# Attention loop in which projections and output products run as pairs in halves of the array's rows

## The chip, the cores and the metric

The kernel runs on one core of a Trainium2 chip. The metric is the device time of one execution in microseconds (us), the median of several runs. A profile of one execution stands beside the times. Its engines are PE (TensorE, matrix products; PEld is its loading of stationary operands), DVE (VectorE), ACT (ScalarE), POOL (GpSimd) and SP (SyncE, which issues most of the DMAs).

## The reference

Four layers, A, B, A, B, act on x (2048 rows of 512), each after a layer norm and with the input added. Layer A is linear attention over learned features. Layer B, which the change touches, cuts the rows into four segments of 512 and attends within each segment, with a memory of the segments before:

```python
for s in range(N):                                   # N = 4 segments, H = 32 heads of 16
    qs, ks, vs = q[:, :, s], k[:, :, s], v[:, :, s]
    logits = einsum("bhqd,bhkd->bhqk", qs, ks) * scale + mask
    a_dot = einsum("bhqk,bhkd->bhqd", softmax(logits), vs)
    pq = phi(qs)                                     # phi(t) = t + 1 if t > 0, else exp(t)
    a_mem = einsum("bhld,bhde->bhle", pq, M) / (einsum("bhld,bhd->bhl", pq, z)[..., None] + 1e-6)
    outs.append(g * a_mem + (1 - g) * a_dot)         # g = sigmoid(beta), one for each head
    pk = phi(ks)
    M = M + einsum("bhld,bhle->bhde", pk, vs)
    z = z + einsum("bhld->bhd", pk)
return concat(outs) @ wo
```

q, k, v are the normed x times wq, wk, wv (512 by 512).

## The kernel before

All products of 512 by 512 weights are split into a high and a low part of each operand, so that each of the four chunks `kc` of the contraction takes three products of 128 rows, 128 columns and 512 moving columns (`mm3`, 12 products a job). A quarter of a job is one `kc`, three products.

Layer B is a loop of steps (`LayerB.steps`). There are 32 values of m a layer, eight for each segment: m picks one of four chunks c of 128 channels (eight heads) and one of two halves of it. Each m takes R = 5 steps, so step k belongs to m = k // 5. A step issues, in this order on each engine:

- `attend(m)`: scores of some blocks into the tile `lg` (two PSUM banks), as pairs of products of 64 rows (`tile_position` 0 and 64) that write different banks; ACT's exponential into a tile of tag `P4` (shown as P); POOL's mask of the diagonal;
- `maxima`, for a later m: pairs of products of 63 rows into `mx` and `my` (a bank each), from which DVE takes row maxima (`mxs`);
- in one step of some m, `read`: the memory's part for a chunk, into `pv` and a bank of tag `g`, which ACT copies to `old` and `upper` (shown as ot and mmq);
- functions put off from the steps before (`later`, `late`), and between them, in steps 0 and 2 of each m, `weighted`: the value sums of the m before, in strips of 32 columns of the array into `pv`, from step 2 on copied by ACT to U; and `update`, the memory's sums of four token blocks, a bank of tag `g`, which DVE adds to the memory. In step 2 the put-off lists come in the other order;
- what the table names for this step.

The tables FIRST (segment 0), GAPS (segments 1 and 2), LAST and FINAL (segment 3 of the first and second layer B) are an order written by hand. An entry `2.3 k3/2~` means: in step 3 of the segment's third m, two quarters of the k projection of chunk 3; a plus sign means the next segment's; `~` puts what DVE does at the job's end off to the next step's list `late`. `q`, `k` are projections, `v` value products, `out` the former segment's output products (four token blocks), `max` turns the maxima and stores them into Q (tile mt), `t` turns features of k to token order, `m` updates the memory, `a` reads it, `x` asks for the rows to which an output is added, `n` and `ln` advance a layer norm (`ln` are its transposes), `w` and `load` bring data, `p`, `pre`, `pt`, `fin` and a bare `v` belong to the end of the layer and to the layer after.

A projection's end (`proj`) is ACT's copy of the high part, DVE's subtraction for the low part, and for the feature map two ACT functions, an exponential and a Relu (`first`, `second`), one or two steps later. A value job ends with an ACT copy, an output with DVE's addition. All of these read the job's bank of tag `g`. There are G = 3 banks of that tag; `lg` has two, `mx`, `my` and `pv` one each, eight in all. Jobs, transposes and the update take a bank of `g` in program order.

`queue_w` loads the next weights of a projection, 512 KB, when one is done; two such tiles (`w4`) are held. `stack(m)` copies projected q and k by six DMAs to the tiles of the scores, in step 0 of the m three before. `Ordered` and `held` keep the order of the program on each engine.

Of the kernel before, what the change touches and what calls it, by code (L numbers as in the profile page):

```python
# [7 lines left out]
F32 = mybir.dt.float32  # L8
# [8 lines left out]
H = 32  # L17
DH = 16
P = 128
# [58 lines left out]


FIRST = """  # L80
0.1 max k2/2 | 0.2 v3/2 | 0.3 k2/2~ | 0.4 v3/2
1.0 m0 | 1.1 max q3/2 | 1.3 q3/2~ | 1.4 t1 k3/1
2.1 max k3/3 | 2.2 m1 w | 2.3 ln~ | 2.4 ln~ ln~
3.1 ln~ max | 3.3 q0+/2 | 3.4 t2 q0+/2~ w
4.0 w | 4.1 max k0+/2 load | 4.2 m2 | 4.3 k0+/1 | 4.4 k0+/1
5.0 n | 5.1 max v0+/4 | 5.2 w | 5.3 q1+/2 n | 5.4 t3 q1+/2~
6.1 max v1+/4 | 6.2 m3 n | 6.3 k1+/2 | 6.4 a0+ k1+/2
7.0 n | 7.1 max q2+/4~ | 7.2 n | 7.3 v2+/2 n | 7.4 t0+ v2+/2
# [12 lines left out]
LAST = """  # L101
0.1 max k2/3~ | 0.2 n | 0.3 k2/1~ v3/2 n | 0.4 a1 v3/2 n
1.0 n | 1.1 max q3/3 n | 1.2 n | 1.3 q3/1~ k3/2 n | 1.4 k3/2~ n
2.1 max out/1 | 2.3 out/2 | 2.4 a2 x0 pre
3.1 max ln~ ln~ | 3.3 pre out/1 ln~ out/1 x1 | 3.4 out/1 ln~
4.1 max out/2~ v/2 | 4.3 pre out/3 x2 | 4.4 a3 out/1~ v/2 x3
5.1 max out/3 | 5.2 out/1 v/1 | 5.3 fin v/1 | 5.4 v/2 pre
6.1 max v/2 | 6.3 fin v/2 | 6.4 v/2
7.1 pt p/3 v/2 | 7.2 v/2 | 7.3 fin v/2 p/3 | 7.4 p/3
"""  # L110
FINAL = """
0.1 max k2/4~ | 0.3 v3/3 | 0.4 a1 v3/1~
1.1 max q3/2 | 1.3 q3/2~ | 1.4 k3/1
2.1 max k3/2 | 2.3 k3/1 out/1 pre | 2.4 a2 out/2 x0
3.0 x1 | 3.1 max | 3.3 pre out/2 | 3.4 out/2
4.1 max out/1~ | 4.3 pre out/2 x2 | 4.4 a3 out/2
5.1 x3 out/2 max | 5.3 fin out/2 | 5.4 pre
6.1 max | 6.3 fin
7.1 pt p/2 | 7.3 p/4 fin | 7.4 p/3
"""  # L120
BEFORE = {-25: "q0 load", -23: "v0", -21: "k0", -18: "n", -17: "v1 n", -16: "n", -15: "n n", -14: "q1 n", -13: "n", -12: "k1 n n", -10: "v2 n", -4: "max q2~", -1: "t0"}


@with_exitstack
def interleave_kernel(ctx, tc, x_in, a_wqkv, a_wphi, a_wo, b_wq, b_wk, b_wv, b_wo, b_beta,
# [15 lines left out]
    def nm(s):  # L141
        uid[0] += 1
        return f"{s}_{uid[0]}"
# [4 lines left out]
    def PS(tag, bufs, shape=(P, 512)):  # L148
        return ps.tile(list(shape), F32, tag=tag, bufs=bufs, name=nm(tag))
# [14 lines left out]
    def behind(i, j):  # L164

        tc.add_manual_dep(i.ins, j.ins.name,
                          mybir.DependencyInfo(mybir.DependencyClass.NoSync, mybir.DependencyReason.DATA),
                          reason="keeps order")

    class Ordered:  # L170

# [36 lines left out]
    def dma(out, in_):  # L208
        return sync.dma_start(out=out.bitcast(F32), in_=in_.bitcast(F32))
# [15 lines left out]
    gated = cp.tile([P, NC, 4], F32, name="gated")  # L225
    ones = cp.tile([32, P], F32, name="ones")
    stats = cp.tile([P, NT, 4], F32, name="stats")
    junk = cp.tile([P, 2, 384], mybir.dt.uint8, name="junk")

    def constants():  # L230
# [776 lines left out]
    class LayerB:  # L1007
# [21 lines left out]

        def values(self, s):  # L1030

            self.vv[s] = []
            yield from v_tile(self.hT[s], self.wv, self.vv[s], ("g", G), (0, 3, 1, 2), True)

        def queue_w(self):

            if self.wnext:
                m, c = self.wnext.pop(0)
                w = wp.tile([P, 2, NC, P], F32R, tag="w4", bufs=2, name=nm("wqk"))
                dma(w, wqk[m][:, c])  # L1040
                self.w4.append(w)

        def proj(self, s, c, m):

            d, hT, w = self.st.setdefault((s, c), {}), self.hT[s], self.w4.pop(0)
            pp = PS("g", G)
            yield from mm3(pp, lambda a, kc: w[:, a, kc, :], lambda b, kc: hT[b][:, kc, :])
            self.queue_w()
# [15 lines left out]
            yield  # L1064

        def at(self, k, f, *a):

# [351 lines left out]

        def out(self, s):  # L1420
            for t in range(4):
                po = PS("g", G)
                yield from self.product(po, s, t, range(NC))

                def end(po=po, t=t):
                    x = self.xq.pop(0)
                    dve.tensor_tensor(out=x, in0=po, in1=x, op=ADD)
                    sync.dma_start(out=self.xdst[4 * s + t], in_=x)
                wait(end)
                yield  # L1430

        def early(self):

# [18 lines left out]
                yield  # L1452

        def opening(self):
            self.w4 = []
            self.wo = []
            self.wnext = [(m, c) for _ in range(NSEG) for c in range(NC) for m in range(2)]
            for _ in range(2):
                self.queue_w()
                yield  # L1460
            self.wv = []
            yield from bring(self.wv, "bwv")
            self.norm0 = self.norm(0)
            next(self.norm0)
            fills = self.start()
            for n in (0, 0, 1, 0, 1, 0, 1, 1, 1, 1, 0, 1, 1, 1, 1, 1, 1, 1, 1):
                yield
                next(self.norm0 if n else fills, None)

        def steps(self, side, after, table_end):  # L1470
# [8 lines left out]
            outs, proj, part = {}, {}, {}  # L1479
            early = self.early()  # L1480

            def do(what, s, k):
                put_off[0] = self.late if what[-1] == "~" else None
# [8 lines left out]
                elif op == "fin":  # L1492
                    if k >= FINAT:
                        self.finish((k - FINAT) // R)
                elif op in ("q", "k", "v", "out", "p"):
                    if op == "p":
                        g = early
                    elif op == "out":
                        if s == 0:
                            return  # L1500
                        g = outs.setdefault(s, self.out(s - 1))
                    elif op == "v":
                        g = after if i is None else val[s]
                    else:
                        g = proj.setdefault((s, i, op), self.proj(s, i, "qk".index(op)))
# [161 lines left out]
```

## Time and profile before

| | us |
|---|---|
| median of 3 runs (1403.53 to 1404.76) | 1403.86 |
| span of the profiled execution | 1401.3 |
| PE busy | 1369.1 |
| DVE busy | 963.9 |
| ACT busy | 810.9 |
| POOL busy | 734.1 |
| first layer B, first to last score product | 292.4 to 713.9 |
| second layer B, first to last score product | 979.0 to 1385.6 |

Matrix products are pipelined and their ends are modelled, so that a busy PE isn't one at its peak: what a product costs is read from one start to the next. The granted clock of TensorE was 1.00 throughout. In the profile's rows, a group stands as output<-inputs by the program's names, with rows by columns of the array and shape, the number of instructions, their busy time, the mean of one, and the idle time of the engine before them with what ended it.

### The profile page before, as it was taken

How to read it: one execution, taken by the hardware profiler on the slowest of the kernel's cores; microseconds unless marked ns; L12 is line 12 of the kernel's file. 1: busy time of each engine (PE TensorE's matmuls, PEld its weight loads, DVE VectorE, ACT ScalarE, POOL GpSimd, SP SyncE). 2: the span in 40 equal slices, each digit the busy share in tenths (PEclk: the TensorE clock that was granted, in tenths of full speed). 3: DMA queues.
4: the chain of work that ended last, by engine and by line, in shares of the span. 5: the costliest groups of instructions: out<-in, count | busy, mean ns of one | idle time of the engine just before them, and what ended most of it. 6: DMA issues, size and time to landing. Idle time of an engine off the chain costs nothing.

```text
span 1401.3 us, 33234 instructions
## 1 busy us (share of the span) xinstructions
PE 1369.1 (98%) x12070; PEld 943.2 (67%) x12070; DVE 963.9 (69%) x3030; ACT 810.9 (58%) x1244; POOL 734.1 (52%) x1073
## 2 busy tenths in 40 slices
PE   9999999999999999999999999999999999999998
PEld 7787778766666666655568887886655666666554
DVE  5766888677667657667647768958776666666674
ACT  5555445447686677566544434553566866765654
POOL 1677755324656656554534346642356565754643
PEclk9999999999999999999999999999999999999999
DMA  5369285645756656567631104855465566565552
GB/s 199 118 216 330 99 280 175 187 122 162 201 131 190 169 137 183 158 171 196 197 134 39 62 31 125 275 162 155 137 172 171 148 178 180 143 172 142 155 158 69
DMA packets 135730, 225.27 MB, mean 161 GB/s; under 512 B 21328, under 2 KB 39888, under 8 KB 135568
## 3 DMA queue, kind: packets, MB, share of 16 engines
q1 hardware_dynamic: 134464, 222.91, 54.2%
q8 instruction: 97, 1.59, 0.5%
q14 instruction: 65, 0.53, 0.1%
q10 hardware_dynamic: 1104, 0.24, 0.1%
HBM read 116.39 MB, written 43.25 MB: 114 GB/s over the span
## 4 chain that ended last, share of the span: by engine, by line
PE 78%; DVE 8%; ACT 5%; POOL 4%; issue 2%; DMA 2%; SPq 0%; DVEq 0%; ACTq 0%; POOLq 0%
PE g L202 47%; PE pv L202 9%; PE lg L202 9%; PE mx L202 4%; PE g L206 3%; PE my L202 3%; ACT P L180 2%; PE lg L206 1%; POOL P L180 1%; POOL tb L180 1%; DVE es L180 1%; POOL tmp L180 1%; DVE junk L180 1%; DVE my L180 1%; DVE mx L180 1%
## 5 line engine op out<-in xcount | busy, mean ns | idle before, releaser
L180 ACT ACTIVATE P<-lg 128x1024 f32<-128x1024 f32 x316 | 324.5, 1027 | 167.5 <-PE lg L202 159.6
L180 POOL TENSOR_SCALAR_AFFINE_SELECT P<-P 128x256 f32<-128x256 f32 (+1 forms) x448 | 190.3, 439 | 388.9 <-ACT P L180 388.1
L180 DVE CUSTOM_DVE_ANT_0 junk<-mx,mask 128x128 uint8<-128x128 f32 (+2 forms) x384 | 146.6, 420 | 101.8 <-PE my L202 72.7
L202 PE MATMUL g<-hh,wqk 128*128 128x512 f32 x512 | 186.3, 411 | 0.7 <-ACT mt L180 0.7
L202 PE MATMUL lg<-e,e 64*128 64x512 f32 (+1 forms) x1010 | 166.0, 386 | 6.4 <-ACT P L180 6.0
L180 DVE CUSTOM_DVE_ANT_0 mx<-mx,mask 128x512 f32<-128x512 f32 x128 | 89.2, 697 | 120.1 <-PE my L202 95.4
L202 PE MATMUL g<-w,oh 128*128 128x512 f32 x508 | 169.2, 414 | 0.5 <-ACT hh L180 0.4
L202 PE MATMUL pv<-P,v 128*32 128x512 f32 (+3 forms) x2048 | 165.5, 439 | 0.6 <-ACT ot L180 0.5
L202 PE MATMUL my<-e,e 63*128 63x256 f32 (+3 forms) x519 | 147.2, 343 | 4.2 <-DVE mxs L180 3.0
L202 PEld LDWEIGHTS lg<-e,e 64*128 64x128 f32 x1010 | 79.9, 184 | 102.9 <-issue 44.9
L202 PE MATMUL mx<-e,e 63*128 63x256 f32 (+3 forms) x519 | 145.9, 334 | 1.9 <-DVE mxs L180 1.6
L180 DVE CUSTOM_DVE_ANT_0 junk<-my,mask 128x128 uint8<-128x128 f32 (+2 forms) x384 | 146.8, 420 | 0.0
L202 PE MATMUL g<-w,hh 128*128 128x512 f32 x448 | 143.9, 402 | 0.3 <-ACT hh L180 0.3
L202 PEld LDWEIGHTS pv<-P,v 128*32 128x32 f32 x2048 | 53.5, 109 | 102.9 <-issue 95.3
L202 PEld LDWEIGHTS g<-hh,wqk 128*128 128x128 f32 x512 | 96.2, 188 | 33.7 <-issue 13.4
L202 PEld LDWEIGHTS g<-w,oh 128*128 128x128 f32 x508 | 87.6, 189 | 30.8 <-issue 13.4
L202 PE MATMUL g<-w,ol 128*128 128x512 f32 x254 | 100.8, 397 | 2.3 <-DVE ol L180 2.2
L180 DVE DVE_READ_ACCUMULATOR2_ANT mxs<- 128x1 f32 x1024 | 100.4, 98 | 0.0
L202 PE MATMUL g<-hl,wqk 128*128 128x512 f32 x256 | 100.3, 392 | 0.0
L202 PEld LDWEIGHTS mx<-e,e 63*128 63x128 f32 (+1 forms) x519 | 90.8, 185 | 10.0 <-DVE mxs L180 5.0
L202 PEld LDWEIGHTS g<-w,hh 128*128 128x128 f32 x448 | 80.3, 188 | 22.6 <-issue 6.0
L202 PEld LDWEIGHTS my<-e,e 63*128 63x128 f32 (+1 forms) x519 | 84.2, 185 | 15.7 <-DVE mxs L180 8.3
(190 smaller groups left out, 2848.2 us busy)
## 6 DMA issues: line engine op xcount, KB each, us to landing
e<-ta SPq DMA_DIRECT2D x384, 128.0 KB
wqk<-wqk SPq DMA_DIRECT2D x64, 512.0 KB
x<-x SPq DMA_DIRECT2D x48, 256.0 KB
xr<-x SPq DMA_DIRECT2D x32, 256.0 KB
x<-xr SPq DMA_DIRECT2D x28, 256.0 KB
tmp<-U SPq DMA_DIRECT2D x56, 128.0 KB
KN<-inv SPq DMA_DIRECT2D x28, 256.0 KB
pq<-tb SPq DMA_DIRECT2D x24, 256.0 KB
```

Of the source, the lines that this page charges most:

```text
L180: i = f(*a, **k)
L202: return held(nc.tensor.matmul(*a, **k))
L206: return held(nc.tensor.transpose(*a))
```

## The change

Projections, value products and output products of layer B become *pairs*. Two jobs run side by side for eight units. In a unit, each of the two jobs does three products of 64 rows for one `kc`, job 0 in one half of the array's rows and job 1 in the other, each to its own bank of `g`. After four units the two swap halves; the sums of both halves of a job go to the same bank. A pair marked `/` does three units, swaps for four and swaps back for one, so that it uses the last chunk's other half late. The two halves of a bank's sum are kept apart in time by `passed`: DVE copies one element (`beat`) at the head of the next step, after the last product of the former half, and the first products of the new half wait for that copy.

In the tables `u/2` means two units of the order PAIRS. `max`, `t`, `m` and most `ln` now stand in steps 0 and 2, beside the value sums. Weights lie in one ring of two slots and are loaded in halves of 64 rows (256 KB) as each half has been used. `stack` moves from step 0 to step 2 from m = 4 on. The jobs' ends stay what they were.

```diff
 GAPS = """
-0.1 max k2/3 | 0.2 n | 0.3 k2/1~ v3/2 | 0.4 a1 v3/2
-1.0 m0 n n | 1.1 max q3/3 | 1.2 n q3/1~ | 1.3 k3/2 | 1.4 t1 k3/2~
-2.1 max out/3 | 2.2 m1 | 2.3 ln ln | 2.4 a2 ln x0
-3.1 max ln out/1~ | 3.3 q0+/3 x1 | 3.4 t2 q0+/1~ k0+/2
-4.1 max k0+/2~ out/1 load | 4.2 m2 | 4.3 out/3~ x2 | 4.4 a3 q1+/4~
-5.0 n | 5.1 max out/3 | 5.3 out/1 v0+/2 n x3 | 5.4 t3 v0+/2 k1+/1
-6.1 k1+/3~ max | 6.2 m3 | 6.3 out/3 | 6.4 a0+ out/1 v1+/2
-7.0 n n | 7.1 max v1+/2 q2+/1 begin | 7.2 n | 7.3 q2+/3~ n N | 7.4 t0+ v2+/4 N
+0.0 u/1 | 0.1 u/2 | 0.2 n max u/1 | 0.3 u/2 | 0.4 a1 u/2~
+1.0 m0 t1 n n u/1 | 1.1 u/2 | 1.2 n max u/1 | 1.3 u/2 | 1.4 u/2~
+2.0 m1 ln | 2.2 ln max ln | 2.3 u/3 | 2.4 a2 u/2 x0 x1
+3.0 ln u/1 | 3.1 u/1 | 3.2 max t2 u/1 | 3.3 u/2 x2 | 3.4 u/2
+4.0 m2 u/1 | 4.1 u/3 load | 4.2 max u/1 | 4.3 u/3 x3 | 4.4 a3 u/3
+5.0 n t3 u/1 | 5.1 u/3 | 5.2 max u/1 | 5.3 u/2 n | 5.4 u/2
+6.0 m3 u/1 | 6.1 u/3 | 6.2 max u/1 | 6.3 u/3 | 6.4 a0+ u/2
+7.0 n n t0+ | 7.1 u/2 begin | 7.2 n max | 7.3 u/2 n N | 7.4 u/2~ N
 """
...
 FIRST = """
+0.1 u/2 | 0.2 max u/2 | 0.3 u/2 | 0.4 u/2~
+1.0 m0 t1 u/1 | 1.1 u/2 | 1.2 max u/1 w | 1.3 u/2 | 1.4 u/2~
+2.0 m1 ln | 2.1 ln~ | 2.2 max ln | 2.3 ln~ w | 2.4 w
+3.0 t2 | 3.1 u/2 w | 3.2 max | 3.3 u/2 | 3.4 u/2
+4.0 m2 | 4.1 u/2 load | 4.2 max | 4.3 u/2 | 4.4 u/2
+5.0 n t3 | 5.1 u/2 | 5.2 max | 5.3 u/2~ n | 5.4 u/2
+6.0 m3 n | 6.1 u/2 | 6.2 max | 6.3 u/2 | 6.4 a0+ u/2~
+7.0 n t0+ u/1 | 7.1 u/2 | 7.2 n max u/1 | 7.3 u/2 n | 7.4 u/2~
...
+PAIRS = (("v3 k2", "q3 k3", "q0+ k0+", "v0+ q1+", "v1+ k1+", "v2+ q2+"),
+         ("v3 k2", "q3 k3", "out out /", "q0+ out", "k0+ out", "v0+ q1+", "v1+ k1+", "v2+ q2+"),
+         ("v3 k2", "q3 k3", "out out /", "out out"))
...
+    def passed():
+
+        if last_half[0] is not None:
+            tick[0] = dve.tensor_copy(beat, bd[0:1, 0:1])
+            sync_on(tick[0], last_half[0])
+            last_half[0] = None
...
+        def pair(self, names, make):
+            jobs = [make(n) for n in names[:2]]
+            po = [PS("g", G) for _ in jobs]
+            order = [(0, 0), (0, 1), (0, 2), (0, 3), (1, 0), (1, 1), (1, 2), (1, 3)]
+            if names[2:]:
+                order = [(0, 0), (0, 1), (0, 2), (1, 0), (1, 1), (1, 2), (1, 3), (0, 3)]
+            halves = [[0, 0], [0, 0]]
+            for step, (turned, kc) in enumerate(order):
+                for n, (a, b) in enumerate(((0, 0), (0, 1), (1, 0))):
+                    for j, (lhs, rhs, _, _) in enumerate(jobs):
+                        h = (j + turned) % 2
+                        rows = slice(64 * h, 64 * h + 64)
+                        i = mm(po[j], lhsT=lhs(a, kc)[rows], rhs=rhs(b, kc)[rows], start=(step == 0 and n == 0),
+                               stop=(step == 7 and n == 2), tile_position=(64 * h, 0))
+                        if step and n == 0 and turned != order[step - 1][0]:
+                            marked(i)
+                        if j and n == 2 and step < 7 and turned != order[step + 1][0]:
+                            last_half[0] = i
...
+                if step == 7:
+                    for p, job in zip(po, jobs):
+                        job[2](p)
+                yield
...
-                if k % R == 0 and 0 <= m < N:
+                if k % R == (0 if m < 4 else 2) and 0 <= m < N:
                     self.stack(m)
+                passed()
```

LAST and FINAL are changed in the same manner.

More of the change, by code (lines that the diff above doesn't have):

```diff
@@ L109 @@
+5.1 v/2 | 5.2 max v/1 | 5.3 fin v/1 | 5.4 v/2 pre
+6.1 v/2 | 6.2 max | 6.3 fin v/2 | 6.4 v/2
 7.1 pt p/3 v/2 | 7.2 v/2 | 7.3 fin v/2 p/3 | 7.4 p/3
@@ L168, in behind, with sync_on, marked @@
                           reason="keeps order")
+    last_half, tick = [None], [None]
+    def sync_on(i, j):
+        tc.add_manual_dep(i.ins, j.ins.name,
+                          mybir.DependencyInfo(mybir.DependencyClass.Sync, mybir.DependencyReason.DATA),
+                          reason="other rows of the array write the same bank")
+    def passed():
[3 more added lines that the diff above has]
+            last_half[0] = None
+    def marked(i):
+        assert last_half[0] is None
+        sync_on(i, tick[0])
     class Ordered:
@@ L227, in interleave_kernel @@
     stats = cp.tile([P, NT, 4], F32, name="stats")
+    beat = cp.tile([1, 1], F32, name="beat")
     junk = cp.tile([P, 2, 384], mybir.dt.uint8, name="junk")
@@ L1030, in values @@
         def values(self, s):
[L1032 to L1041, printed above, removed]
-        def proj(self, s, c, m):
[L1045 to L1048, printed above, removed]
+            v = sp.tile([P, 4, VROW], F32, tag="v", bufs=2, name=nm("v"))
@@ new lines, in queue_w, with whole @@
+        def queue_w(self, n, h):
+            if n < len(self.wnext):
+                m, c = self.wnext[n]
+                rows = slice(64 * h, 64 * h + 64)
+                dma(self.ring[rows, n % 2], wqk[m][rows, c])
+        def whole(self, job):
+            lhs, rhs, end, used = job
+            po = PS("g", G)
+            yield from mm3(po, lhs, rhs)
+            used(0)
+            used(1)
+            end(po)
+            yield
[10 more added lines that the diff above has]
+                        h = (j + turned) % 2
+                        rows = slice(64 * h, 64 * h + 64)
+                        i = mm(po[j], lhsT=lhs(a, kc)[rows], rhs=rhs(b, kc)[rows], start=(step == 0 and n == 0),
[4 more added lines that the diff above has]
+                            last_half[0] = i
+                for j, job in enumerate(jobs):
+                    h = (j + turned) % 2
+                    halves[j][h] += 1
+                    if halves[j][h] == NC:
+                        job[3](h)
+                if step == 7:
+                    for p, job in zip(po, jobs):
+                        job[2](p)
+                yield
@@ L1421, in out, with end, added @@
             for t in range(4):
[L1422 to L1430, printed above, removed]
+                def end(po, t=t):
+                    def added():
+                        x = self.xq.pop(0)
+                        dve.tensor_tensor(out=x, in0=po, in1=x, op=ADD)
+                        sync.dma_start(out=self.xdst[4 * s + t], in_=x)
+                    wait(added)
+                yield (lambda a, kc, t=t: self.oT[s, kc][a][:, t * P : (t + 1) * P],
+                       lambda b, kc: self.wo[b][:, kc, :], end, lambda h: None)
         def early(self):
@@ L1478, in steps, with job, units @@
             val = [self.values(s) for s in range(NSEG)]
-            outs, proj, part = {}, {}, {}
+            outs = [None] + [self.out(s) for s in range(NSEG - 1)]
+            whole, part = {}, {}
             early = self.early()
+            def job(name, s):
+                s += name[-1] == "+"
+                name = name.rstrip("+")
+                if name == "out":
+                    return next(outs[s])
+                if name[0] == "v":
+                    return next(val[s])
+                return self.proj(s, int(name[1]), "qk".index(name[0]))
+            def units():
+                for s in range(NSEG):
+                    for names in PAIRS[0 if s == 0 else 1 if s < NSEG - 1 else 2]:
+                        yield from self.pair(names.split(), lambda name: job(name, s))
+            units = units()
             def do(what, s, k):
@@ L1494, in do @@
                         self.finish((k - FINAT) // R)
-                elif op in ("q", "k", "v", "out", "p"):
+                elif op == "u":
+                    for _ in range(int(quarters)):
+                        next(units)
+                elif op in ("q", "k", "v", "p"):
                     if op == "p":
                         g = early
[L1498 to L1503, printed above, removed]
-                    else:
-                        g = proj.setdefault((s, i, op), self.proj(s, i, "qk".index(op)))
+                    elif i is None:
+                        g = after
+                    else:
+                        if (s, what) not in whole:
+                            whole[s, what] = self.whole(job(what, s))
+                        g = whole[s, what]
                     n = int(quarters) if quarters else (3 if op == "p" else 4) - part.pop(op, 0) % 4
```

61 lines of the change are left out of this document (35 added, 26 removed).

## The prediction

> **What bounds the kernel now.** I read the page first (shares and the chain that ended last), then busy time by stretches, the waits, and the order of instructions inside one pass of the attention loop.
>
> ```profile
> span 1401.3 us, 33234 instructions
> PE 1369.1 (98%) x12070; PEld 943.2 (67%) x12070; DVE 963.9 (69%) x3030; ACT 810.9 (58%) x1244; POOL 734.1 (52%) x1073
> PE 78%; DVE 8%; ACT 5%; POOL 4%; issue 2%; DMA 2%; SPq 0%; DVEq 0%; ACTq 0%; POOLq 0%
> L180 ACT ACTIVATE P<-lg 128x1024 f32<-128x1024 f32 x316 | 324.5, 1027 | 167.5 <-PE lg L202 159.6
> ...
> 400.00:505.00 105.00, 104.36 (x858) 65.22 (x857) 69.04 (x277) 73.06 (x109) 61.66 (x99) 1.00 0.62 171
> ...
> PEld lg L202 <- ACT P L180: 6.9, 22, 0.6
> ```
>
> TensorE is busy and carries 78% of the chain; in a stretch of the loop (columns PE, PEld, DVE, ACT, POOL) it has 104.36 of 105 us, ACT 73.06, DVE 69.04. In 400 to 610 us its weight loads for the scores waited 6.9 us for ACT's exponentials: almost nothing waits. The 316 exponentials are one for nearly every step of the loop (5 steps for each m, 32 m a layer, two layers). So the time is the PE's own sequence, and in that sequence I look for what isn't multiplication:
>
> ```profile
> 446.50 0.48 PE L202 MATMUL g<-hh,wqk 128*128 128x512 f32 x1
> 446.82 0.39 PE L202 MATMUL g<-hl,wqk 128*128 128x512 f32 x1
> 447.05 0.63 PE L202 MATMUL g<-hh,wqk 128*128 128x512 f32 x2
> 447.52 0.39 PE L202 MATMUL g<-hl,wqk 128*128 128x512 f32 x1
> ...
> 448.44 0.40 PE L202 MATMUL g<-w,ol 128*128 128x512 f32 x1
> 448.77 0.56 PE L202 MATMUL lg<-e,e 64*128 64x256 f32 x4
> 449.17 0.40 PE L202 MATMUL mx<-e,e 63*128 63x512 f32 x1
> 449.50 1.28 PE L202 MATMUL pv<-P,v 128*32 128x384 f32 x16
> ...
> 450.60 0.48 PE L202 MATMUL g<-v,tb 128*32 128x34 f32 x32
> ...
> 454.41 0.28 PE L202 MATMUL mx<-e,e 63*128 63x256 f32 x1
> 454.53 0.28 PE L202 MATMUL mx<-e,e 63*128 63x256 f32 x1
> 454.65 0.59 PE L202 MATMUL pv<-tb,mem 64*68 64x512 f32 x1
> ...
> 455.08 0.59 PE L202 MATMUL pv<-tb,mem 64*68 64x512 f32 x1
> ```
>
> From start to start a full-array product of 512 columns takes 0.23 us (446.82 to 447.05). The first after half-array work takes 0.32 (446.50 to 446.82), the last before it 0.33 (448.44 to 448.77). Leaving a mode costs 0.10, entering the next 0.09: a change of mode is worth 0.19 to 0.20 us, whatever lies on either side. The scores and maxima of a step take 0.73 with both changes (448.77 to 449.50), 0.5 without; half of the value sums 1.1 (449.50 to 450.60), 1.2 with the drain; a read of the memory 2 x 0.43 (454.65 to 455.08).
> The Trainium skill's "TensorEngine Tiling (Array Packing)", Key Properties, says that changing the tiling mode drains the engine; the trace agrees with 0.10 for the drain and shows another 0.09 for the first weight load, which no longer lies behind a product.
>
> **The change, part by part.**
>
> *Modes.* Before, in each of the five steps of an m the PE enters half-array work (scores, maxima) and leaves it: 10 changes. After, steps 1, 3 and 4 hold only half-array work, since projections, values and output products are pairs of halves: 6 fewer. The transpose of the maxima now follows the value sums in step 2 (1 more), and token transposes and norm columns follow value sums in some steps (0.6 more on average). Tables FIRST, GAPS, GAPS and the part of LAST that has units cover 8+8+8+4 = 28 m of a layer: 28 x 4.4 = 123 fewer, 246 in both, x 0.20 = 49 us saved.
>
> *The pairs themselves.* A unit is 3 pairs of half products for two jobs, in place of 3 full products for one: equal only if two halves of 512 columns run in the time of one full product. No row shows such a pair in mid-stream. Below: 0.12 for a pair of 256 columns (454.41 to 454.53) doubled is 0.24, less its fixed part (the full 512 takes 0.23). Above: 0.33 (449.17 to 449.50), which has a drain in it. Less 0.10 that is 0.23. I take 0.23, cost nothing; 0.24 would cost 0.01 x 3 x 416 units = 12 us, 0.33 would cost 125.
>
> *Banks.* This decides it. Tag g has three PSUM banks, and a pair holds two from its first unit to its evacuation; the third serves maxima transpose, tokens, columns, memory update and one half of the read. A new pair needs two at once, so at least one bank of the pair just ended must have been emptied, and both jobs end at the same unit. The evacuations, in 400 to 610 us:
>
> ```profile
> L180 ACT ACTIVATE P<-lg 128x1024 f32<-128x1024 f32 x77 | 79.1, 1028 | 42.1 <-PE lg L202 40.7 <-POOL stats L180 0.9 <-PE my L202 0.3
> L180 ACT ACTIVATE tb<-g 128x512 f32<-128x512 f32 x28 | 15.5, 599 | 0.1
> L180 ACT ACTIVATE U<-pv,share 128x512 f32<-128x512 f32 x16 | 11.0, 689 | 6.9 <-PE pv L202 6.5 <-DMA den<-mmq 0.4
> L180 ACT CAST ta<-g 128x512 fp32r<-128x512 f32 x16 | 9.4, 586 | 9.4 <-PE g L202 9.1 <-DMA den<-ot 0.2
> L180 ACT ACTIVATE ot<-pv,bd 68x512 f32<-68x512 f32 x8 | 5.5, 684 | 0.1
> L180 ACT COPY v<-g 128x512 f32<-128x512 f32 x8 | 4.7, 589 | 5.0 <-PE g L202 5.0
> ...
> L180 DVE CUSTOM_DVE_ANT_0 mx<-mx,mask 128x512 f32<-128x512 f32 x30 | 20.9, 698 | 37.2 <-PE my L202 28.6 <-PE mx L202 8.4
> L180 DVE TENSOR_TENSOR ta<-g,ta 128x512 fp32r<-128x512 f32 x16 | 11.0, 690 | 7.2 <-ACT tb L180 7.2
> L180 DVE TENSOR_TENSOR xr<-g,xr 128x512 f32<-128x512 f32 x8 | 5.4, 674 | 0.6 <-PE g L202 0.6
> ```
>
> A projection's bank is free after ACT's copy (0.59), DVE's subtraction (0.69) and, for the feature maps, two ACT functions (0.60 each), which the code issues one or two steps later; an output's bank after DVE's addition (0.67). Take T as the issue of a pair's last product; its result is there at T+0.2 (a product shows 0.39 against 0.23 from start to start). Table GAPS, step 4.2, where pair k0+/out follows q0+/out: ACT copies q0+ to T+0.8, takes the step's exponential (1.03) to 1.8, U (0.69, value sums end at 1.7 on PE) to 2.7, then the two functions to 3.9; DVE subtracts to 1.5 and adds the output to 2.2. The third bank holds the maxima, whose copy comes after the functions. Two banks are free at T+3.9; the PE is there after scores (0.5), value sums (1.2) and the transpose (0.2), at T+1.9. It waits 2.0 us.
> The other starts, in the same way: 5.1, the output's add behind the subtraction at 2.2 against scores only at 0.5, 1.7 (1.2 in the last GAPS segment, whose k has no feature map). 6.0, q1+ free at 3.6 behind two copies, exponential and functions, PE there at 2.1, 1.6. 6.4, the read's own bank free after two ACT passes of 0.68 at 4.4, PE there at 1.4, 3.0 (1.0 in the last GAPS segment). 1.0, token copy and update hold the free banks, 1.7. 2.3 and 3.3, 0.5 each. Inside pairs, t2 behind the maxima in the same bank at 3.2, 1.2; columns behind the update at 2.0, 0.5. A GAPS segment pays about 12.7 and 10.1, FIRST 5.5 (1.0, 2.0, 4.3, 6.0, 7.0), LAST 3: 31 a layer, 62 in all. Step 2.1 has no unit any more, so that ACT's row of two copies, four functions and two exponentials (1.2+2.4+2.1 = 5.7 us) shows at 2.2 as a wait for the scores' bank, some 2 us a segment, 11 in all. Off that come waits for DVE's maxima that the longer steps cover; now these are
>
> ```profile
> PEld my L202 <- DVE mxs L180: 8.3, 22, 0.5
> PEld mx L202 <- DVE mxs L180: 5.0, 10, 1.5
> ...
> PE my L202 <- DVE mxs L180: 3.0, 13, 0.3
> ```
>
> 16 in all, which I take as covered: 62 + 11 - 16 = 57. Bounds: 0 (if nothing of it stands on the PE's way) and 90 (each of the 52 starts as dear as the mean of 4.2 and 5.1, 1.8).
> Skill and row point the same way here only in part: the Trainium skill's "TensorEngine Tiling (Array Packing)", Gotcha 1, warns that row tiling increases PSUM pressure, and that speaks against this change. No run here has shown it yet; by that page alone there is no price.
>
> *Swap of halves.* The second half's first product waits for a one-element DVE copy, issued at the next step's head, which waits for the first half's last product. 29 swaps a layer. It is queued behind the former step's maxima,
>
> ```profile
> 449.60 0.70 DVE L180 CUSTOM_DVE_ANT_0 mx<-mx,mask 128x512 f32<-128x512 f32 x1 [1.15 <-PE mx L202]
> ```
> ```profile
> 447.00 0.28 DVE L180 CUSTOM_DVE_ANT_0 junk<-mx,mask 128x128 uint8<-128x128 f32 x1
> ...
> 448.37 0.08 DVE L180 DVE_READ_ACCUMULATOR2_ANT mxs<- 128x1 f32 x1
> ```
>
> 1.45 us (447.00 to 448.45), begun 0.83 into a step where no subtraction stands ahead (449.60 after the scores' 448.77), and any subtraction issued there; what is queued behind it are that step's maxima, which need the PE's new scores anyway. Steps last 2.0 or more and scores (0.5) go ahead of the waiting product: 0. Bounds: 0 and 0.69 (one subtraction in the way) x 58 = 40 us.
>
> *Queues.* The 64 weight loads of 512 KB become 128 of 256 KB, each waiting on SP for its half's last use.
>
> ```profile
> L180 SPq DMA_DIRECT2D wqk<-wqk x64: 319/326/1242, 183.2 to 1301.9; - x64
> L180 SPq DMA_DIRECT2D e<-ta x384: 526/596/2325, 250.5 to 1346.5; - x192
> ```
>
> 64 x 0.33 = 21 us more of SP issue, spread over 800 us; a half is used at least four steps later. The six stacking loads of an m (0.6 each, 3.6 us) move from step 0 to 2 and still have four steps (8 us or more) to the maxima that read them; the maxima's store moves past one step of four. I take 0; were the stacks late by 1 us in each of 50 m, 50 us.
>
> *Sum.* Of the profiled 1401.3 us: -49 +57 = +8, 1409.3. The runs' median 1403.86 is 2.6 above that span, so 1412.
>
> **The rivals.**
> 1. Faster: the bank waits are smaller. For it: 49 us over 52 pairs is 0.94 us a pair; a mean wait below that decides for a gain, and mine is 57/52 = 1.1, so little is needed. ACT still has 30% free. Against: the waits follow from orders on ACT and DVE that are written out. With half of the waits, -49 +28: 1383; with none, 1355.
> 2. Nothing measurable: gain and waits within 2.8 us of each other, 1404.
> 3. Pairs of halves run slower than a full product, slower by 20% being 0.046 x 3 x 416 = 57 us more, 1469. Against it the 0.12 of the pair with 256 columns.
> The Trainium skill's "TensorE: Matmul & The Clock Gate", Part 3, gives a speedup of 3.07 for four row tiles, not 4, so packed tiles need not run free; the rows of 256 columns here don't show such a loss.
> 4. The swap waits for DVE after all: up to 40 us more, 1440.
>
> **How the numbers follow.** Two results differ from no change here by 0.2%, 2.8 us. My forecast, slower by bank waits, 0.41; rival 1, 0.37; rival 2, 0.11; rival 3, 0.05; rival 4, 0.06. Slower 0.41+0.05+0.06 = 0.52, same 0.11, faster 0.37. The likeliest case alone: 1407 to 1430. The range goes down into rival 1 (waits at a quarter, -49 +14, is 1369; I stop at 1372) and up to rival 4, 1440.
>
> **What would show it.** Right: in the waits, PE or its loads on tile g wait for ACT tb, ACT ta, ACT mt and DVE xr some 50 us where now nearly none stands; step 4.2 of a gap segment near 4.6 us with a hole before its first unit; steps 1 and 3 near 2.0 us without 0.32 to 0.33 intervals; half products 0.23 apart; stretches like 400 to 610 longer, the first segment's not. Wrong: unit starts without holes (rival 1), half pairs beyond 0.24 apart (rival 3), products released by the DVE tile beat (rival 4), maxima released by a DMA into e (stacks late).

## The result and the profile after

The changed kernel takes 1470.5 us, the median of four runs (1468.2 to 1470.8), against 1403.7 us before: a ratio of 1.0469, 95% interval [1.0455, 1.0484]. The forecast of 1412 (1372 to 1440) had the sign and missed the size: +66.8 us where +8 was forecast. Times here and below are medians of four runs, but of three for the kernel with full products, one bank at a time, whose fourth run took 2542.36 us and isn't counted.

The page after, three of its lines (the third is the granted TensorE clock in 40 slices of the span):

```profile
span 1468.9 us, 35919 instructions
PE 1381.1 (94%) x13318; PEld 998.7 (68%) x13318; DVE 976.4 (66%) x3088; ACT 816.2 (56%) x1244; POOL 736.9 (50%) x1073
PEclk9999999998999999999999999999999999999998
```

The same stretch of the loop as before (columns PE, PEld, DVE, ACT, POOL, then the clock, DMA share and GB/s), and below it seven stretches of the first segment, four from step 2 of m = 2 on and three from step 2 of m = 4 on; the half clock begins in m = 3 and in m = 4:

```profile
400.00:505.00 105.00, 97.56 (x979) 67.66 (x976) 65.20 (x258) 67.22 (x97) 57.12 (x92) 0.97 0.62 154
...
327.26:330.67 3.41, 3.24 (x32) 1.87 (x33) 1.98 (x7) 1.67 (x4) 2.81 (x4) 1.00 0.76 182
330.67:334.08 3.41, 1.97 (x14) 1.18 (x13) 2.30 (x10) 2.94 (x4) 0.99 (x3) 1.00 0.84 274
334.08:340.91 6.83, 6.61 (x32) 3.24 (x32) 3.27 (x14) 2.20 (x3) 0.83 (x2) 0.50 0.75 216
340.91:344.32 3.41, 3.41 (x37) 2.00 (x33) 3.21 (x13) 1.64 (x3) 0.97 (x3) 1.00 0.07 16
354.56:357.97 3.41, 2.63 (x22) 1.07 (x14) 2.88 (x12) 2.76 (x6) 0.77 (x2) 1.00 0.91 237
357.97:364.80 6.83, 5.14 (x28) 4.40 (x30) 1.87 (x10) 3.15 (x5) 5.96 (x6) 0.50 0.52 134
364.80:368.21 3.41, 3.41 (x35) 1.91 (x35) 1.55 (x5) 1.37 (x2) 2.70 (x7) 1.00 0.38 94
```

In 105 us of the loop PE lost 6.8 us of its 104.36 busy ones. The seven short rows show something that the profile before has nowhere: the clock column goes from 1.00 to 0.50, stays there for 6.83 us and comes back. In the half clock 32 products take 6.83 us, as many as in 3.41 us two rows earlier (their sizes are mixed; the spacing of one kind of product is shown further down).

What PE, or its weight loads, waited for in the whole span (engine, tile, what released it; total us, times, longest). PEld and PE wait for the same event one behind the other, so such rows are not to be added up:

```profile
PEld lg L225 <- ACT P L203: 28.1, 44, 1.9
...
PEld g L225 <- ACT tb L203: 17.9, 22, 2.5
PE lg L225 <- DMA e<-mt: 17.2, 12, 4.2
...
PE lg L225 <- ACT P L203: 14.5, 27, 1.6
...
PE g L225 <- ACT tb L203: 10.9, 13, 2.2
...
PEld g L225 <- DVE xr L203: 7.0, 13, 1.6
...
PEld g L225 <- DVE ta L203: 6.6, 6, 1.3
...
PEld my L225 <- DVE mxs L203: 5.7, 16, 0.5
...
PE my L225 <- DVE mxs L203: 5.2, 24, 0.3
PEld mx L225 <- DVE mxs L203: 5.2, 13, 0.7
```

The first row is no loss by itself, for the weight loads waited longer for ACT's exponentials before the change; the products themselves waited less:

```profile
PEld lg L202 <- ACT P L180: 36.6, 100, 1.1
...
PE lg L202 <- ACT P L180: 6.0, 16, 0.9
```

The row of e<-mt is new: scores wait for a DMA, the store of the maxima (mt) into the tile e that the scores read.

To add up the loops I took PE's timeline from the first to the last score product of each loop (two more us for the last step), counted every product with its spacing at full clock (0.229 for 512 columns, full or a pair of halves; 0.117 for 256, and so on), and every change of mode with 0.20. What is left is "rest": waits, and what the half clock costs. Clock is an account of that second part: the full-rate time of the products that began at half clock, which is what the half rate adds to them, and no proof that the run would be that much shorter without. Sums over both loops, in us; the kernels from the third on are the experiments that follow:

| kernel | loops | products | mode changes | rest | of it clock |
|---|---|---|---|---|---|
| before | 832.0 | 667.7 | 641: 128.2 | 36.1 | 0 |
| after | 898.3 | 667.7 | 390: 78.0 | 152.7 | 28.1 |
| full products, alternating, two banks | 915.1 | 667.7 | 723: 144.6 | 102.8 | 23 |
| full products, one bank at a time | 891.9 | 667.7 | 723: 144.6 | 79.7 | 15.4 |
| features from SBUF | 873.4 | 667.7 | 390: 78.0 | 127.7 | 15.4 |
| the same full products, max in step 1 | 867.3 | 667.7 | 721: 144.2 | 55.5 | 12.5 |
| after, max in step 1 | 903.4 | 667.7 | 451: 90.2 | 145.5 | 35.1 |
| after, max in step 1, features from SBUF | 855.3 | 667.7 | 451: 90.2 | 97.5 | 15.3 |

The loops are 66.3 us longer, nearly all of the difference between the runs: 50 us fewer for modes, 117 more of rest.

### The profile page after: what moved, and what is told of

The parts are those of the page before. It is cut to its first block, busy times and chain, and to the rows that moved or that the text cites. A ratio compares the mean times of both kernels' runs of the same rounds, so it can differ in the third digit from the quotient of the medians.

```text
span 1468.9 us, 35919 instructions
## 1 busy us (share of the span) xinstructions
PE 1381.1 (94%) x13318; PEld 998.7 (68%) x13318; DVE 976.4 (66%) x3088; ACT 816.2 (56%) x1244; POOL 736.9 (50%) x1073
## 5 line engine op out<-in xcount | busy, mean ns | idle before, releaser
L225 PE MATMUL g<-hh,wqk 64*128 64x512 f32 (+1 forms) x944 | 299.8, 410 | 18.6 <-ACT tb L203 6.2
L225 PE MATMUL g<-w,hh 64*128 64x512 f32 (+1 forms) x656 | 221.8, 415 | 0.3 <-ACT hh L203 0.3
L225 PE MATMUL g<-w,oh 64*128 64x512 f32 (+1 forms) x700 | 194.3, 417 | 4.7 <-ACT tb L203 4.2
L225 PE MATMUL lg<-e,e 64*128 64x512 f32 (+1 forms) x1010 | 163.0, 349 | 31.7 <-DMA e<-mt 17.2
L225 PEld LDWEIGHTS g<-hh,wqk 64*128 64x128 f32 (+1 forms) x944 | 156.0, 188 | 48.4 <-ACT tb L203 10.3
L225 PE MATMUL g<-hl,wqk 64*128 64x512 f32 (+1 forms) x472 | 162.4, 398 | 0.0
L225 PEld LDWEIGHTS lg<-e,e 64*128 64x128 f32 x1010 | 106.1, 189 | 71.3 <-ACT P L203 28.1
L225 PEld LDWEIGHTS g<-w,hh 64*128 64x128 f32 (+1 forms) x656 | 118.8, 189 | 19.8 <-issue 2.5
L225 PE MATMUL g<-w,hl 64*128 64x512 f32 (+1 forms) x328 | 129.6, 395 | 0.0
L225 PEld LDWEIGHTS g<-w,oh 64*128 64x128 f32 (+1 forms) x700 | 103.0, 188 | 31.3 <-issue 8.2
L225 PE MATMUL g<-w,ol 64*128 64x512 f32 (+1 forms) x350 | 115.5, 393 | 2.6 <-DVE ol L203 2.6
```

Of the source, the lines that this page charges most:

```text
L225: return held(nc.tensor.matmul(*a, **k))
```

## The experiments

My theory at first was the prediction's: the waits for the banks of pairs eat the gain. The rivals were the new places in the tables (of `max`, `t` and the stacking loads) and, once seen, the clock.

**Without pairs, with the new tables.** In the first kernel the two jobs of a pair alternate as full-array products and still hold two banks to a common end; in the second they run one after the other, each with its own bank and end (only the pairs marked `/` stay together).

```
-            for step, (turned, kc) in enumerate(order):
...
+            for step in range(8):
+                j, kc = step % 2, step // 2
...
+                    mm(po[j], lhsT=lhs(a, kc), rhs=rhs(b, kc), start=(kc == 0 and n == 0), stop=(kc == 3 and n == 2))
```

The second has in place of the line with `j`:

```
+                j, kc = (step % 2, step // 2) if together else (step // 4, step % 4)
+                if po[j] is None:
+                    po[j] = PS("g", G)
...
+                    end(po[j])
```

> The tables, the pairs and their common end stay; each unit does three full-array products for one of the two jobs in turn, without halves and without the swap. It tells apart what half products and swaps cost. Theory (banks): both banks are still held and still end together, so the waits stay and the changes of mode come back, 123 a layer at 0.2 us, less what longer steps hide: 1490 to 1520 us. Rival (half products or the swap's wait for DVE are what costs): the cost goes, 1404 to 1440 us.

Measured: 1486.64 us, 1.0586 [1.0569, 1.0602], just below what the theory gave. Against the changed kernel the mode changes are back (66.6 us), but the time grows by only 16, because rest is 50 us less (the table's third row): a good part of what the pairs save in modes turns into waiting.

> As the former, but the two jobs of a pair run one after the other, each takes its bank when it starts and ends by itself (only the pair marked / stays together). It tells apart holding two banks from the new tables. Theory (banks): most waits for banks of g and most of the clock's drops go, the changes of mode are back, the late stores of the maxima stay: 1410 to 1440 us. Rival (the new places of max, t and stack cost the time): as slow as the former, 1480 us or more.

Measured: 1464.98 us, 1.0454 [1.0415, 1.0494], between the two expectations and some 22 us below the kernel that holds two banks (in that one PE also waited 7.3 us for weights, which both jobs free only near the end). The row below is from another run of it:

> The run with full products and one bank at a time again, for its trace: 1463 to 1475 us. Theory (banks): waits of products on g for ACT tb below 5 us, the rest of the loss in steps 2.0 to 2.2 and in late stores of the maxima. Rival: waits on g as in the changed kernel.

Measured: 1462.92 us. It has

```profile
PE lg L225 <- DMA e<-mt: 17.8, 14, 3.0
```

and hardly a wait for ACT's features of a projection (0.9 us on PE). So my theory falls in its main claim: with the pairs and most of their common ends gone, the kernel is still about 59 us slower than before, from what else the change brings, the new tables above all (the places of the stacking loads and the ring of weights are in it too): 16 us of mode changes (723 against 641) and 44 of rest, late stores and the clock among it. Put the pairs on top and modes fall by 67 us (723 to 390), but rest grows by 73. Of the first, the prediction had the mode changes, inside its net of 4.4 an m, and 11 us of rest; the other 33 it lacked.

**The bank waits by themselves.** The features of q and k read the high part that ACT has just written to SBUF, not the bank, so that the bank is free after the copy and DVE's subtraction (the features are then those of the rounded high part).

```
-                    act.activation(e, pp, AF.Exp)
+                    act.activation(e, hi.bitcast(F32), AF.Exp)
```

> The changed kernel, but the two ACT functions of a feature map read the copy of the high part in SBUF and no longer the bank (so the features come from the high part alone); same work on every engine. Theory (banks held by the late functions): waits of products on g for ACT tb go, and some of the clock's drops with them: 1420 to 1445 us. Rival (ACT itself has no time left): 1460 to 1475 us.

Measured: 1447.89 us, 1.0312 [1.0295, 1.0329], between the two expectations. The waits of g for tb fall to

```profile
PE lg L225 <- DMA e<-mt: 22.0, 14, 4.7
...
PEld g L225 <- ACT tb L203: 1.6, 2, 1.0
```

from 17.9, while the scores' wait for the store grows from 17.2 to 22.0. 22.6 us are gained; in the table rest falls by 25, of which 12.7 is the clock, at half rate for 41 us of the loops in place of 68. The bank waits are real, and with the clock a third of the loss. Taking the output's addition ahead of the projection's subtraction on DVE gave nothing:

```
-                    for p, job in zip(po, jobs):
-                        job[2](p)
+                    for j in sorted(range(2), key=lambda j: names[j] != "out"):
+                        jobs[j][2](po[j])
```

> The changed kernel, but where a pair of a projection and an output ends, DVE adds the output first and then subtracts for the projection, which has to wait for ACT's copy anyway. Theory (the start of step 5.1 waits for the output's bank behind that subtraction): 1 to 1.5 us at each of four starts, 1464 to 1468 us. Rival (that start waits for something else): no difference, 1468 to 1473 us.

Measured: 1468.97 us, 1.0462 [1.0446, 1.0477], not to be told from the changed kernel.

**The late store.** PE at the longest of these waits, ACT's copy of the turned maxima, and SP's queue in the same time (start, duration, instruction):

```profile
640.59 0.50 PE L225 MATMUL lg<-e,e 64*128 64x512 f32 x2 [4.21 <-DMA e<-mt]
```
```profile
632.53 0.25 ACT L203 ACTIVATE mt<-g 16x128 fp32r<-16x128 f32 x1
```
```profile
633.19 4.55 SPq L203 DMA_DIRECT2D e<-ta x6
638.23 0.33 SPq L203 DMA_DIRECT2D inv<-dn  x1
638.65 0.60 SPq L203 DMA_DIRECT2D e<-mt  x1
```

The maxima are ready at 632.78, but the six stacking loads, 0.76 us each, now stand ahead of the store in step 2 of the same m (and a small load, inv, behind them), so that it is issued only at 638.65; the scores start 2 us after that. Three edits went at that. The store on ACT's queue:

```
-            (sync if s else act).dma_start(out=Q[63:P:64].bitcast(F32), in_=mt.bitcast(F32))
+            act.dma_start(out=Q[63:P:64].bitcast(F32), in_=mt.bitcast(F32))
```

> The changed kernel, but the store of the turned maxima is always issued by ACT, not by SP behind the stacking loads that now stand in the same step. Theory (the store is late because SP issues six stacking loads first): the 17 us in which scores wait for a DMA into e go, and a drop of the clock with them: 1447 to 1456 us. Rival (the maxima themselves are late, or ACT's issue delays the exponentials): 1463 to 1475 us.

Measured: 1471.51 us, 1.0483 [1.0465, 1.05]. Most of the late stores go, and the wait is handed on to ACT's row:

```profile
PEld lg L225 <- ACT P L203: 43.1, 55, 2.2
...
PE lg L225 <- DMA e<-mt: 5.5, 4, 2.4
```

The stacking loads behind the table's entries, so behind the store:

```
-                if k % R == (0 if m < 4 else 2) and 0 <= m < N:
+                if k % R == 0 and 0 <= m < 4:
                     self.stack(m)
...
                 for w in what:
                     do(w, s, k)
+                if k % R == 2 and 4 <= m < N:
+                    self.stack(m)
```

> The changed kernel, but from m = 4 on the six stacking loads are issued behind the step's table entries, so behind the store of the turned maxima. Theory (the store is late only because SP issues the stacking loads first): waits of scores for a DMA into e fall from 17 us to a few, and nothing is put on ACT as in the run that moved the store there: 1445 to 1458 us. Rival (SP's queue as a whole is late, or the stacks are then late for the maxima): 1465 to 1480 us.

Measured: 1493.22 us, 1.062 [1.0589, 1.065], slower than either expectation. Now the stacks are late, and the maxima wait:

```profile
PE mx L225 <- DMA e<-ta: 17.8, 17, 3.6
...
PEld mx L225 <- DVE mxs L203: 16.3, 16, 4.3
```

And the stacking back in step 0 where its projections are ready by then:

```
-                if k % R == (0 if m < 4 else 2) and 0 <= m < N:
+                if k % R == (2 if m >= 4 and m % 8 in (0, 2, 4) else 0) and 0 <= m < N:
```

> The changed kernel, but the stacking loads stay in step 2 only for three of eight m (those whose projections end too late for step 0) and go back to step 0 for the others. Theory (SP has too little slack in step 2 for both the stacking loads and the store of the maxima): waits of scores for a DMA into e fall from 17 us to under 6, waits of maxima for a DMA into e stay near none: 1452 to 1462 us. Rival (the store is late for reasons of its own, such as the later place of max): 1466 to 1474 us.

Measured: 1468.63 us, 1.047 [1.0445, 1.0496]. The twelve late stores stay (17.0 us): all but 1.2 us of them stand at m = 13, 15, 21, 23 and 25, just where the loads wait for fresh projections and had to stay in step 2. So this run moved none of the loads that hold a store up, and doesn't tell theory from rival.

**The clock.** Products whose sums nobody reads fill holes of the first segment (13 us of PE a layer in the first kernel, 5 in the second; each filler shows as two products of 0.43). The edit is abridged, and what stands behind # is a note:

```
-2.0 m1 ln | 2.1 ln~ | 2.2 max ln | 2.3 ln~ w | 2.4 w
-3.0 t2 | 3.1 u/2 w
+2.0 m1 ln | 2.1 ln~ | 2.2 max ln | 2.3 ln~ w y/3 | 2.4 w y/3    # second: y/1, y/1
+3.0 t2 y/1 | 3.1 u/2 w
...
+    4.3 z/8 u/2                                                 # second: z/3
```

> The changed kernel with added products in the long waits of segment 0 (steps 2.3, 2.4, 3.0 and 4.3, 15 a layer of 64 rows and 512 columns, 6.5 us a layer), into banks that nobody reads. Theory (the clock falls to half after such waits and the products after them run at half rate): the drops in m = 3 and 4 of both layers vanish, and the time does not grow although work is added: 1458 to 1468 us. Rival (the clock costs nothing because PE waits anyway): the added work shows, 1472 to 1484 us.

Measured: 1477.67 us, 1.0525 [1.0507, 1.0542], in the rival's range, though the drops in m = 3 and 4 are gone in both layers.

> As the run with added products, with fewer: 2 x 3 products of 0.43 us in steps 2.3, 2.4, 3.0 and 2 x 3 in 4.3, 5.2 us a layer in place of 12.9. Theory (the drop of the clock costs up to 2 to 3 us after each of two waits a layer): below the changed kernel although work is added, 1462 to 1468 us, with no drop in m = 3 and 4. Rival (the drop costs nothing): 1470 to 1478 us.

Measured: 1464.51 us, 1.0441 [1.0421, 1.0461]. The first kernel in two stretches that had half the clock in the changed kernel, and the second kernel in the first of them:

```profile
334.00:341.00 7.00, 7.00 (x57) 4.21 (x58) 4.06 (x15) 2.98 (x4) 0.88 (x3) 1.00 0.60 175
358.00:365.00 7.00, 7.00 (x44) 4.38 (x43) 1.20 (x7) 1.27 (x2) 5.66 (x8) 1.00 0.23 62
```
```profile
334.00:341.00 7.00, 6.81 (x42) 3.62 (x41) 3.36 (x14) 2.52 (x3) 0.41 (x1) 0.76 0.64 185
```

Full clock in both for the first kernel; the second still has one window of 3.41 us at half clock in m = 3 of the first layer. With 10 us of useless work more, the second kernel is 6 us faster than the changed one by the medians, 4 by the ratios to the kernel before, whose intervals just touch; its clock loss is 15 us, not 28. That the added work doesn't show at all is clear, the gain is at the edge of the noise. Filling the holes takes away the falls that stood behind them: there the low clock follows from the holes, and it is a cost of its own, if the small gain is taken as real. Elsewhere falls came and went with the shifted times, so that the first kernel still had 55 us at half clock in its loops, against 68.

**Together.** The features from SBUF and the addition first, by the edits shown above; on top of them the first kernel has the stacking loads behind the table's entries, the second the stacking loads back in step 0 where they can be.

> Features from the high part in SBUF, the output added first, and the stacking loads behind the store of the maxima, together. If the three causes are separate, their gains add: 22 us for the first, 15 to 23 for the store, 4 for the order of ends, and some of the clock's drops: 1415 to 1430 us. If one wait only takes another's place: 1435 to 1448 us.

Measured: 1478.0 us, 1.0533 [1.0512, 1.0555], slower than either expectation: the late stacks again (maxima waited 18.4 us for them).

> Features from the high part in SBUF, the output added first, and the stacking loads back in step 0 where they can. If the causes are separate their gains add to the 22 us of the first: 1425 to 1440 us. If they only hand the wait on: 1444 to 1452 us.

Measured: 1446.41 us, 1.0296 [1.0265, 1.0327], not to be told from the features alone.

**The place of max.** Open was now what it is in the tables that costs the first 59 us. The entry `max` goes back from step 2 of each m to step 1, as before the change, and the store with it, ahead of the stacking loads; first with full products one bank at a time, then with the pairs, then with the pairs and the features from SBUF. One line of the tables:

```
-4.0 m2 u/1 | 4.1 u/3 load | 4.2 max u/1 | 4.3 u/3 x3 | 4.4 a3 u/3
+4.0 m2 u/1 | 4.1 max u/3 load | 4.2 u/1 | 4.3 u/3 x3 | 4.4 a3 u/3
```

> Full products, one bank at a time, and in all tables the maxima's turn and store (max) back from step 2 of each m to step 1, as in the kernel before; all else as in the changed kernel. Theory (the tables' new place of max, with the stacking loads ahead of it on SP and a change of mode more, makes up most of what full products with the new tables cost over the kernel before): against 1462.9 the late stores go (17.8 us) and some 80 changes of mode (16), and part of the low clock with them: 1422 to 1442. Rival (max's place is not it, the rest of the tables is): 1455 to 1466.

Measured: 1439.31 us, 1.0238 [1.0212, 1.0263]. As expected in time, and no score waits for a store; but the mode changes stayed (721 against 723), so all of the 24 us between the two profiled runs came from rest, 3 of them clock.

> The changed kernel with max back in step 1 of each m, ahead of that step's half-array pairs. Theory: 17 us of late stores go and perhaps 5 to 10 of the low clock, but a turn between half-array work costs two changes of mode in each of some 56 m, 22 us: 1462 to 1478, with hardly a product waiting for a DMA into e. Rival (stores late whatever step asks for them): the changes of mode come on top, 1485 to 1495.

Measured: 1472.0 us, 1.0467 [1.0433, 1.0501]: no gain, as the theory had it, but not for its reason. The mode changes cost 12 us and not 22. The rest of what the stores gave back went into a new wait, of the transposes of the maxima (L229) for the bank of the pair that ended a step before, and into more low clock (35 us):

```profile
PEld g L225 <- ACT tb L203: 15.2, 20, 2.0
...
PEld g L229 <- ACT tb L203: 13.9, 12, 1.6
```

With the same tables the full products of the run before are 33 us faster than these pairs.

> As the run before, and the feature map reads the high part from SBUF instead of the bank. Theory (the two costs are separate places of the same steps, so their ends add): some 22 us less than the run before, 1438 to 1458. Rival (what one frees, the next wait takes): within 8 us of the run before.

Measured: 1428.95 us, 1.0164 [1.0143, 1.0186], 43 us below the run before and 14 below the lower end of what was expected.

```profile
span 1426.9 us, 35933 instructions
PE 1370.4 (96%) x13318; PEld 994.8 (70%) x13318; DVE 976.4 (68%) x3088; ACT 815.3 (57%) x1244; POOL 736.0 (52%) x1073
...
PEld g L225 <- ACT tb L203: 1.5, 2, 1.0
...
PEld g L229 <- ACT tb L203: 0.9, 4, 0.3
```

Each edit alone gave 22.6 and -1.5 us (the latter not to be told from nothing), both together 41.5. They act as two waits in a row: with the store out of the way PE runs into the bank (the 13.9 us above), and with the bank free it still runs into the store (22.0 us, where it was 17.2). In the table, rest without the clock falls by 12 us with the features alone, by 14 with max alone and by 42 with both. The clock's loss of 15 us isn't a joint effect, for the features alone had it too; max alone had 35.

This is the best version that I found, and the kernel before remains faster: against it this one has 38 us less of mode changes and 61 more of rest, 15 of them clock. Full products in the same tables but without the features from SBUF stand 10 us above it. How far the pairs by themselves are ahead with the features from SBUF in both wasn't run.

## Why the prediction was wrong

*Modes*: right. 49 us were forecast, 251 changes fewer x 0.20 = 50 measured.

*The pairs themselves*: right. Half products run side by side, 0.23 us from pair to pair:

```profile
404.62 0.39 PE L225 MATMUL g<-w,hh 64*128 64x512 f32 x1
404.62 0.39 PE L225 MATMUL g<-hh,wqk 64*128 64x512 f32 x1
404.85 0.39 PE L225 MATMUL g<-w,hh 64*128 64x512 f32 x1
404.85 0.39 PE L225 MATMUL g<-hl,wqk 64*128 64x512 f32 x1
405.08 0.39 PE L225 MATMUL g<-w,hl 64*128 64x512 f32 x1
```

Rival 3 is out: that its 1469 us is the measured time is chance. A loss such as the Trainium skill's "TensorE: Matmul & The Clock Gate", Part 3, gives for four row tiles isn't seen with two halves.

*Swap of halves*: right at 0. The copies took 142 ns by the median (shortest, median and longest in the row), and DVE waited for PE before them; nobody waited for them:

```profile
L203 DVE COPY beat<-bd x58: 84/142/144, 304.2 to 1411.6; 1x1 f32<-1x1 f32 x58
its engine sat idle before it (us, times) until:
  PE g L225: 27.8, 38
who waited for it (us, times):
```

*Banks*: right in kind, too large in size. From the holes on PE I put the pair starts at some 21 us a layer, 42 in all, against 62. Step 4.2 of a gap segment lasted 4.24 to 4.31 us against 4.6, its wait 1.4 against 2.0; 6.0 0.4 against 1.6 (a late store ahead of it, 1.4 us in the first of these segments, had already given ACT time). The one at 4.3 in the first segment was larger, 3.5 us, where the forecast had 5.5 for that segment's five starts together, and here the wait turns into the next one: ACT's second pair of functions ends late, PE stands still, and what starts then runs at half the clock:

```profile
359.66 0.79 PE L225 MATMUL g<-hh,wqk 64*128 64x512 f32 x1 [2.19 <-ACT tb L203]
...
360.25 0.62 PE L225 MATMUL g<-hl,wqk 64*128 64x512 f32 x1
360.68 0.62 PE L225 MATMUL g<-hh,wqk 64*128 64x512 f32 x1
361.10 0.62 PE L225 MATMUL g<-hh,wqk 64*128 64x512 f32 x1
```

The pairs are 0.42 apart (360.68 to 361.10) where 0.23 is full speed. At ACT's row, steps 2.0 to 3.0, PE stood some 26 us, but the kernel before had some 13 us of rest of its own in steps 2.0 to 3.2, where its layer norm stands, so that the growth is near the 11 of the forecast. What I took off for maxima that longer steps cover (16) did not come: the three rows of waits for mxs, 8.3, 5.0 and 3.0 us before, are 5.7, 5.2 and 5.2 after. (As loads and products wait one behind the other, these rows should not have been added in the first place; and the upper bound of the bank waits, 52 starts of 1.8, is 94 and not 90.)

*Queues*: the first step that failed. To take 0 for the maxima's store overlooked that it now stands on SP behind six loads of 0.76 us in the same step, and that those loads themselves wait for projections at some m. PE waited 17 us for it directly. The bound that I gave was on the stacks being late, not the store behind them: I counted what the move does to the moved transfers and not to the one that is queued behind them.

*The clock*: the second, and the larger. No term of the sum had it; every duration was taken at clock 1.00, because the kernel before never left it. By the account above it cost 28 us, a term as large as any other that was missed. One of the signs named beforehand fails by it: the first segment, which was to stay as long as it was, went from 99.8 to 108.3 us, with two falls of the clock in it (the rows 334.08 and 357.97 above).

Together: bank starts 42, ACT's row 13 more than before, stores 17 and clock 28 are 100 of the 117 us of rest; some 17 stay open. The first two are read from the holes on PE and are rough where a hole lies in a low-clock stretch; the wait for the stores is a row, the clock an account from the trace. So against the forecast of 57 the banks were 20 less and ACT's row about right; the 16 taken off did not come, and stores and clock, taken at nothing, make 45. The experiments bear out that banks, stores and clock cost time, not each figure: features from SBUF 22.6, the store's place with them 19 more. Both edits together still leave 25 us over the kernel before, and what in the tables holds these isn't shown.

## What to carry to other kernels

When a change bundles an engine's work, price not only the engine's own sequence but what the bundle does to the others: two results due at once are two evacuations in a row, and a load that is moved is put ahead of everything behind it on its queue. Where TensorE is the bound, a hole of 2 us may cost more than 2 us, if the clock halves behind it as it did here; look at the clock column before the waits. And when an edit at the largest wait gives nothing, look for a second wait right behind it, and take away both before you drop either.

## What the runs showed of the hardware

The clock fell in eleven episodes in the loops of the changed kernel, nine of 6.83 us and two of 3.41, 68 us together. All 24 changes of clock in that profile lie on one grid of 3.413 us. In the 3.41 us ahead of each fall, the products (at their full-rate time) filled 0.16 to 0.40 of the window, in nearly all other windows more than 0.41; the row 330.67:334.08 above is such a window, with PE busy 1.97 of 3.41 us by the modelled ends. The share is no sharp threshold: two windows at 0.38 and 0.40 were not followed by a fall, nor was one at 0.33 in the kernel before, though a few records of products may be missing there. The Trainium skill's "TensorE: Matmul & The Clock Gate", Part 1, describes this gate, with a free-running window of 3413 ns and half rate after an idle one. The grid and the half rate agree with the trace; but here the engine was far from idle in the window ahead of a fall.
